# K and Q evacuated as interleaved 16-bit head pairs, with a new order per segment type, in a segment-recurrent attention kernel

## The chip, the cores and the metric

The kernel runs on one core of a Trainium2 chip. A core has TensorE (PE; its weight loads are shown as PEld), VectorE (DVE), ScalarE (ACT), GpSimd (POOL) and SyncE (SP), which issues the DMAs here. The metric is the device time of one execution in microseconds. All three runs of the kernel before lie within 0.6% of one another.

## The reference

A layer norm, a recurrent attention over segments with a memory, a residual, and a feed-forward block behind a second and third layer norm:

```python
B, S, Dm = 1, 2048, 512;  H, Dh = 32, 128;  M, seg = 8, 32
mem = mem0
for s in range(64):
    h = concat([mem, xs[s]])                       # 8 + 32 rows
    q, k, v = (einsum('btd,dhe->bhte', h, W) for W in (Wq, Wk, Wv))
    p = softmax(where(mask, q @ k^T * Dh**-0.5, -1e9))
    o = einsum('bhte,hed->btd', p @ v, Wo)
    mem = o[:, :8]                                 # the recurrence
    outs.append(o[:, 8:])
h1 = x + concat(outs)
z = layernorm(layernorm(h1))
out = h1 + gelu(z @ w1 + b1) @ w2 + b2             # F = 1792
```

Everything is 16-bit float outside of PSUM and the softmax. Each segment needs the eight memory rows of the one before it, so the 64 segments are a chain.

## The kernel before, in words

The four projection weights (4 MB each) stay in SBUF. Tokens come in 16 blocks of 128 rows, that is of four segments. A segment's 40 rows are worked on in two portions. Portion A is 32 rows: the first 24 tokens of the segment and the 8 memory rows; it must wait for the recurrence. Portion B is the last 8 tokens of each of the four segments of a block: 32 rows which do not depend on the memory and are projected once for a block, ahead of time. All 32 heads are held as two halves r = 0, 1 of 16 heads, and matmuls use the array as four column groups of 32, each for another part of the head dimension (`one_pass`, line 589: four chunks of four matmuls with 512 moving columns for one half of one projection).

What a segment s does, by the names of the parts in the order table:

- `K0, K1, Q0, Q1`: K and Q of portion A. Their result in PSUM has tokens on partitions. `kq_T` (line 631) is a DVE transpose of 32 x 32 blocks, from PSUM to the tile `kqT`, 4-byte floats. From there `k_seg` casts to `KALL` (16 bit, line 611); `q_seg` copies the memory queries scaled into `ZC` (line 612) and the 24 token queries scaled into `QA` (GpSimd, line 646). `zc_fill` (GpSimd, line 654) puts the B queries beside the memory queries in `ZC`.
- `V`: both halves together (`two_passes`, lines 601 and 367: the second half uses the weights that the first loaded), cast to `VS`.
- `SC0, SC1`: scores of the memory and B queries, into a PSUM bank prefilled with a mask (`prefill`, line 705; `sc_mm`, line 721); `sc_softmax` then runs maximum (729), exponential `EC` on ScalarE (733), reciprocal `rsc` (736), product `PC` (739) and transpose `PTC` (740).
- `PV0, PV1`: probabilities times V (751, 755), copied to `OT` (memory rows) and `OTB` (B rows).
- `WO`: the output projection in eight units of eight matmuls (832). A DVE transpose to `TT` (844) and two additions (838) make the next segment's memory rows in `hT`: this closes the recurrence.
- `SA` and `PVA`: attention of the 24 tokens, not in the recurrence: scores (779), softmax `SA`, `PA`, transpose `PTA` (789 to 795), product with V (804) in the next segment, output rows with the next but one's `WO`.
- `F0, F1`: portion B of the next block: its K in segment type 0 (s mod 4), its Q in type 1, its V in type 2, which also goes through DRAM into the layout `VBD`; in type 3 the output projection of the block before (`wo_B`). `TR` holds the transposes of layer norm (`ln1`) and residual (`nat`), which are there in types 0 and 1.

One PSUM group of four banks (`quad`) and four single banks (4 to 7, table `BANK`) are used by hand.

The order of TensorE's work is the written table `ORDER`, one for every segment (the first has `START`). All other operations are placed by a planner in the program: `Sched.schedule` sorts them by the length of the rest of their chain plus a `BONUS` per kind, then puts each into its engine's line at the earliest free time by its estimated duration (`dur`, `t_dve`, `t_act`, `t_pool`). For TensorE it also models the fetch of instructions (`FETCH_N`, `FETCH_US`). An operation made with `either` may run on several engines and takes the one that ends first by the estimates, where DVE is charged `LEAN` more. The estimates set nothing but the order and the engine; at run time each engine goes through its list in order and waits for semaphores.

After segment 63 the feed-forward block runs (lines 1083 to 1134), 128 x 512 matmuls in four rounds; its weights overwrite `WK` and its tiles `WQ` and `WV`.

Of the kernel before, what the change touches and what calls it, by code (L numbers as in the profile page):

```python
# [17 lines left out]
HOP = {"pe": 0.21, "act": 0.06, "dve": 0.05, "pool": 0.08, "sp": 2.0}  # L18
SWITCH = 0.1
OVERLAP = {"act": 0.1, "dve": 0.07, "pool": 0.05, "sp": 0.0}  # L20
DMA_SEMS = 100
FETCH_N, FETCH_US = 256, 3.5
HALVES = ("kqT", "KA", "ZCm", "QA", "VS", "nmc", "EC", "rsc", "PC", "PTC", "OTm", "KB", "QTB", "VSB")
BONUS = {"EC0": 40, "EC1": 40, "KA0": -2.1, "KB0": 7.39, "KB1": 40, "OTm0": -2.89, "OTx": -40, "PC0": 23.1, "PTC1": 40, "QA1": -40, "QTB0": 0.74,
# [3 lines left out]
LEAN = 0.36  # L28
# [3 lines left out]
ORDER = (("K0", 0, 1), ("K1", 0, 1), ("K0", 1, 2), ("K1", 1, 2), ("K0", 2, 99), ("K1", 2, 3), ("Q0", 0, 1), ("K1", 3, 99), ("Q0", 1, 99),  # L32
         ("Q1", 0, 99), ("V", 0, 1), ("SC0", 0, 99), ("V", 1, 99), ("SC1", 0, 99), ("F0", 0, 99), ("TR", 0, 99), ("PV0", 0, 99), ("SA", 0, 99),
         ("WO", 0, 3), ("PV1", 0, 99), ("WO", 3, 99), ("F1", 0, 99), ("PVA", 0, 99))
BANK = dict(K0=7, K1=5, Q0=4, Q1=7, V0=4, V1=5, SC0=6, SC1=7, F0=6, F1=4, FB=6, SA=4, WO=5)
# [23 lines left out]
class Sched:  # L59
# [79 lines left out]
    @staticmethod  # L139
    def lat(p, o):  # L140
        if p.is_dma:
            return HOP["sp"]
        if p.eng == "pe" and o.eng == "pe":
            return 0.0
        return HOP[p.eng]

    def schedule(self):
# [25 lines left out]
        def push(o):  # L173
            heapq.heappush(heap, (-o.rank - BONUS.get(o.kind, 0.0), pos[o], o.gidx, o))
# [13 lines left out]
        fetched, blocks = 0, [0.0]  # L188
        starts = {e: [] for e in ENGINES}
        for o in order:  # L190
# [5 lines left out]
            if o.eng == "pe":  # L196
                if o.prev is not None:
                    q = o.prev
                    t = max(t, q.start + q.dur + (SWITCH if q.mode != o.mode else 0.0))
                fetched += o.ni  # L200
                while fetched >= FETCH_N * len(blocks):
                    t = max(t, blocks[-1] + FETCH_US)
                    blocks.append(t)
                o.start = t
                lines["pe"].append(o)
                continue
# [150 lines left out]

MC, MR, MF = 1, 2, 3
# [14 lines left out]
def t_dve(n):  # L373
    return 0.16 + 1.042e-3 * n


def t_act(n, ps=True):
    return (0.14 if ps else 0.2) + 0.886e-3 * n


def t_pool(n):
    return 0.16 + 2.1e-3 * n


def build_kernel(nc, A_x, A_mem0, A_Wq, A_Wk, A_Wv, A_Wo, B_w1, B_b1, B_w2, B_b2, out):
# [3 lines left out]
    with st:  # L389
# [20 lines left out]
        kqT = sb("kqT", [P, 6, 512], F32)  # L410
        KALL = sb("KALL", [P, 4, H, 32])
        QTB = sb("QTB", [P, 2, H, 32])
        ZC = sb("ZC", [P, 2, H, 32])
        QA = sb("QA", [P, H, 32])
# [90 lines left out]
        S.op("dve", lambda e: e.memset(QA[:], 0.0), writes=[("QA", r) for r in range(2)], dur=0.5)  # L505
# [39 lines left out]
        def ln1(tb):  # L545
# [4 lines left out]
            S.op("dve", lambda e: e.bn_aggr(ag, stt[:, i, :]), reads=[("st", i)], writes=[("ag", i)], dur=0.15)  # L550
# [3 lines left out]
                 reads=[("xr", tb % XR), ("ag", i), ("rs", i)], writes=[("xn", i)], dur=0.38)  # L554
# [29 lines left out]
        def one_pass(lhs, reads, W, key, r, bank, rhs):  # L584

            for cc in range(DC):
# [4 lines left out]
                S.op("pe", f, reads=[(key, r, cc)] + reads, writes=[("ps", bank)], dur=0.215, mode=MC, ni=8)  # L591

        def two_passes(lhs, reads, W, key, banks, rhs):

            for cc in range(DC):
# [9 lines left out]
                S.op("pe", f, reads=[(key, r, cc) for r in range(2)] + reads, writes=[("ps", b) for b in banks], dur=0.43, mode=MC, ni=12)  # L605

        def copy2(out, src, n, ps_=True, scale_=None):

            fast = 1.0 if ps_ else 0.5
            if scale_ is None:  # L610
                return {"act": (lambda e: e.copy(out, src), t_act(n, ps_)), "dve": (lambda e: e.tensor_copy(out, src), 0.16 + 1.042e-3 * n * fast)}  # L611
            return {"act": (lambda e: e.mul(out, src, scale_), t_act(n, ps_)),  # L612
                    "dve": (lambda e: e.tensor_scalar(out, src, scale_, None, ALU.mult), 0.16 + 1.042e-3 * n * fast)}
# [16 lines left out]
        def kq_T(i, bank):  # L630
            S.op("dve", lambda e: e.transpose(kqT[:, i, :], ps[bank][:, :]), reads=[("ps", bank)], writes=[("kqT", i)], dur=t_dve(512) + 0.02)  # L631
            return kqT[:, i, :].rearrange("p (h t) -> p h t", h=16)

        def k_seg(s, r, bank):
            par, i, h0 = s % 2, r, 16 * r
            src = kq_T(i, bank)
            S.either(copy2(KALL[:, par, h0:h0 + 16, :], src, 512, False), reads=[("kqT", i)], writes=[("KA", par, r)])

        def q_seg(s, r, bank):
            par, i, h0 = s % 2, 2 + r, 16 * r  # L640
            src = kq_T(i, bank)
            z = ZC[:, par, h0:h0 + 16, :]
            dst = bass.AP(z.tensor, z.offset, [list(z.ap[0]), [64, 8], [48, 2], [1, MEM]])
            sz = src[:, :, NA:SEG].rearrange("p (a b) t -> p a b t", b=2)
            S.either(copy2(dst, sz, 128, False, scale), reads=[("kqT", i)], writes=[("ZCm", par, r)])
            S.op("pool", lambda e: e.tensor_scalar(QA[:, h0:h0 + 16, 0:NA], src[:, :, 0:NA], scale, None, ALU.mult),  # L646
                 reads=[("kqT", i)], writes=[("QA", r)], dur=1.19)

        def zc_fill(s):
# [3 lines left out]
            src = QTB[:, bk % 2, :, 8 * sg:8 * sg + 8].rearrange("p (a b) t -> p a b t", b=2)  # L653
            S.op("pool", lambda e: e.tensor_copy(dst, src), reads=[("QTB", bk % 2, q) for q in range(2)], writes=[("ZCb", par)], dur=0.45)

# [3 lines left out]
        def kq_B(bk, qk, r, bank):  # L659
            W, key = WKQ[qk]  # L660
            one_pass(*pack_b(bk), W, key, r, bank, cols_kq)
            src = kq_T(4 + r, bank)
            h0 = 16 * r
            if qk == 0:
                S.either(copy2(KALL[:, 2 + bk % 2, h0:h0 + 16, :], src, 512, False), reads=[("kqT", 4 + r)], writes=[("KB", bk % 2, r)])
            else:
                S.either(copy2(QTB[:, bk % 2, h0:h0 + 16, :], src, 512, False, scale), reads=[("kqT", 4 + r)], writes=[("QTB", bk % 2, r)])

        def v_B(bk, r, bank):
            one_pass(*pack_b(bk), WV, "WV", r, bank, cols_v)  # L670
            S.either(copy2(VSB[:, :, r, :], ps[bank][:, :].rearrange("p (i e) -> p i e", i=4), 512), reads=[("ps", bank)], writes=[("VSB", r)])
# [36 lines left out]
        def sc_mm(s, r, bank):  # L708
# [4 lines left out]
            def f(e):  # L713
                for i in range(4):
                    for j in range(4):
                        h = 16 * r + 4 * j + i
                        b0 = (reg * H + h) * 32 + 8 * sg - 8 * i
                        a0 = (par * H + h) * 32
                        rhs = bass.AP(ka.tensor, ka.offset + a0, [list(ka.ap[0]), [b0 - a0, 2], [1, 32]])
# [5 lines left out]
                 writes=[("ps", bank)], dur=0.13, mode=MC, ni=32)  # L725
# [467 lines left out]
```

## Time and profile before

| | |
|---|---|
| median of 3 runs | 899.82 us |
| lowest and highest | 896.92, 902.28 us |
| profiled execution: span from the first to the last instruction (no other time of it is given) | 898.3 us |
| busy: PE, DVE, ACT, POOL | 822.1, 652.2, 521.9, 223.7 us |
| HBM read, written | 28.98, 8.39 MB |
| mean granted TensorE clock | 0.991 |

A busy share is an average over three stages: the load of the weights with the first segment, the chain of segments, and the feed-forward block. Matmuls are pipelined and their ends are modelled, so TensorE's share says little on how much of its time is free. For the chain of segments, the useful number is the distance of the starts of two segments, and what the chain of waits passes through between them. A row of that chain reads: start, duration, engine, tile and line, number of instructions. A row of the groups reads: line, engine, operation, output and input tiles, shapes, count, then busy time and mean duration in ns, then idle time ahead of it and what ended it.

### The profile page before, as it was taken

To read this page: it belongs to the slowest core of one execution; us is meant where nothing else is said; L and a number is where in the kernel's file an instruction comes from. 1 tells how busy PE (TensorE), PEld (TensorE's weight loads), DVE (VectorE), ACT (ScalarE), POOL (GpSimd) and SP (SyncE) were. 2 spreads that over 40 slices of the span, in tenths; PEclk is the share of its full clock that TensorE was granted. 3 is DMA by queue.
4 is the path that set the end of the run, shared out by engine and by line. 5 is a ranking of instruction groups with operands and counts; after the bars stand their busy time and mean duration, and the time that the engine had idled before them with its cause. 6 is when DMAs were issued, how large, how long until landed. Compare 5 with 4: busy or idle time off the path is not lost.

```text
span 898.3 us, 47685 instructions
## 1 busy us (share of the span) xinstructions
PE 822.1 (92%) x22271; PEld 433.7 (48%) x21261; DVE 652.2 (73%) x1801; ACT 521.9 (58%) x1520; POOL 223.7 (25%) x305
## 2 busy tenths in 40 slices
PE   2578999999999999999999999999999998889998
PEld 0134455555545555545555545555555554454443
DVE  2258788888788988897888888878797878741111
ACT  1246665657566757666757655667665656534442
POOL 3023222223232323232222222222222222223100
PEclk9789999999999999999999999999999999999999
DMA  8860000000001010101010101010101110421000
GB/s 335 285 218 10 4 15 22 19 25 15 28 10 33 9 31 12 27 16 27 16 27 16 28 15 27 9 28 9 27 10 27 34 27 10 150 77 47 24 24 23
DMA packets 35301, 40.42 MB, mean 45 GB/s; under 512 B 2452, under 2 KB 31004, under 8 KB 35100
## 3 DMA queue, kind: packets, MB, share of 16 engines
q1 hardware_dynamic: 35100, 37.38, 12.8%
q8 instruction: 170, 2.79, 1.3%
q14 instruction: 31, 0.25, 0.1%
HBM read 28.98 MB, written 8.39 MB: 42 GB/s over the span
## 4 chain that ended last, share of the span: by engine, by line
PE 72%; ACT 15%; DVE 6%; DMA 3%; issue 3%; SPq 1%; POOL 0%; DVEq 0%
PE ps L589 27%; PE ps L832 15%; ACT VS L611 7%; PE ps L601 7%; PE ps L367 6%; PE ps L1083 5%; PE quad L1090 5%; ACT EC L733 4%; ACT OT L611 3%; DVE kqT L631 2%; PE quad L804 2%; PE quad L751 2%; DMA WQ<-in_A_Wq_dram 1%; DMA xr<-in_A_x_dram 1%; PE ps L721 1%
## 5 line engine op out<-in xcount | busy, mean ns | idle before, releaser
L646 POOL TENSOR_SCALAR QA<-kqT 128x384 bf16<-128x384 f32 x128 | 150.0, 1172 | 488.1 <-PE ps L589 320.0
L631 DVE STREAM_TRANSPOSE kqT<-ps 128x512 f32<-128x512 f32 x320 | 217.9, 710 | 29.2 <-PE ps L589 19.2
L832 PE MATMUL ps<-WO,OT 128*32 128x256 bf16 x4224 | 153.6, 274 | 17.6 <-issue 6.2
L611 ACT CAST KALL<-kqT 128x512 bf16<-128x512 f32 x160 | 98.6, 618 | 80.3 <-DVE kqT L631 78.9
L589 PE MATMUL ps<-WK,hT 128*32 128x512 bf16 x2048 | 133.3, 380 | 3.9 <-DVE hT L838 3.6
L589 PE MATMUL ps<-WQ,hT 128*32 128x512 bf16 x2048 | 134.0, 382 | 0.0
L611 ACT CAST OT<-quad 128x128 bf16<-128x128 f32 (+1 forms) x176 | 80.1, 455 | 82.9 <-PE quad L755 46.8
L832 PEld LDWEIGHTS ps<-WO,OT 128*32 128x32 bf16 x4224 | 95.7, 96 | 49.5 <-ACT OT L611 33.5
L601 PE MATMUL ps<-WV,hT 128*32 128x512 bf16 x1024 | 100.7, 383 | 1.0
L367 PE MATMUL ps<-WV,hT 128*32 128x512 bf16 x1024 | 99.8, 380 | 0.0
L589 PEld LDWEIGHTS ps<-WQ,hT 128*32 128x32 bf16 x2048 | 54.7, 98 | 57.7 <-DVE kqT L631 2.4
L733 ACT ACTIVATE EC<-ps,nmc 128x64 f32<-128x64 f32 x256 | 78.0, 313 | 0.8 <-DVE nmc L729 0.8
L611 ACT CAST VS<-ps 128x512 bf16<-128x512 f32 x127 | 68.2, 589 | 10.4 <-PE ps L367 3.4
L589 PEld LDWEIGHTS ps<-WK,hT 128*32 128x32 bf16 x2048 | 49.0, 96 | 48.4 <-DVE hT L838 3.3
L1086 ACT ACTIVATE WQ<-ps,b1t 128x512 bf16<-128x512 f32 x56 | 38.5, 688 | 57.2 <-PE ps L1083 56.8
L705 ACT COPY ps<-maskCF 128x128 f32<-128x128 f32 x122 | 32.8, 269 | 65.1 <-DVE kqT L631 34.6
L844 DVE STREAM_TRANSPOSE TT<-ps 128x256 f32<-128x256 f32 x66 | 29.3, 444 | 41.8 <-PE ps L832 41.8
L1134 DVE TENSOR_TENSOR WV<-quad,WV 128x512 bf16<-128x512 f32 x16 | 11.0, 690 | 66.7 <-PE quad L1090 66.7
L601 PEld LDWEIGHTS ps<-WV,hT 128*32 128x32 bf16 x1024 | 27.3, 97 | 60.9 <-DVE kqT L631 29.9
L721 PEld LDWEIGHTS ps<-KALL,ZC 128*32 128x32 bf16 x2048 | 34.3, 97 | 44.4 <-ACT ZC L612 35.1
L1090 PE MATMUL quad<-WK,WQ 128*128 128x512 bf16 x217 | 53.7, 379 | 0.9 <-DVE xr L878 0.5
L733 ACT ACTIVATION_READ_ACCUMULATOR EC<-ps,nmc 128x1 f32 x256 | 52.3, 204 | 0.0
(107 smaller groups left out, 1210.7 us busy)
## 6 DMA issues: line engine op xcount, KB each, us to landing
WV<-in_A_Wv_dram SPq DMA_DIRECT2D x4, 1024.0 KB, 6.9
WK<-in_A_Wk_dram SPq DMA_DIRECT2D x4, 1024.0 KB, 8.0
v_last<-VSB SPq DMA_DIRECT2D x64, 64.0 KB, 2.1
WQ<-in_A_Wq_dram SPq DMA_DIRECT2D x4, 1024.0 KB, 8.5
VBD<-v_last SPq DMA_DIRECT2D x64, 64.0 KB
WO<-in_A_Wo_dram SPq DMA_DIRECT2D x4, 1024.0 KB, 9.1
WK<-in_B_w_dram SPq DMA_DIRECT2D x2, 1792.0 KB, 13.2
xr<-in_A_x_dram SPq DMA_DIRECT2D x16, 128.0 KB, 2.8
```

Of the source, the lines that this page charges most:

```text
L367: return e.add_instruction(mybir.InstMatmult(name="I-%d" % (4000000 + _kept[0]), engine=mybir.EngineType.PE, start_tensor_calc=start, stop ...
L589: ins = e.matmul(ps[bank][32 * j:32 * j + 32, :], lhs(cc), rhs(W, r, cc, j), start=(cc == 0), stop=(cc == DC - 1), tile_position=(0, 32 * j))
L601: ins = e.matmul(o, l, m, start=(cc == 0), stop=(cc == DC - 1), tile_position=(0, 32 * j))
L611: return {"act": (lambda e: e.copy(out, src), t_act(n, ps_)), "dve": (lambda e: e.tensor_copy(out, src), 0.16 + 1.042e-3 * n * fast)}
L631: S.op("dve", lambda e: e.transpose(kqT[:, i, :], ps[bank][:, :]), reads=[("ps", bank)], writes=[("kqT", i)], dur=t_dve(512) + 0.02)
L646: S.op("pool", lambda e: e.tensor_scalar(QA[:, h0:h0 + 16, 0:NA], src[:, :, 0:NA], scale, None, ALU.mult), reads=[("kqT", i)], writes=[("Q ...
L721: ins = e.matmul(ps[bank][32 * j:32 * j + 32, 64 * sl:64 * sl + 64], ZC[:, par, h, :], rhs, start=False, stop=(i == 3), tile_position=(0, ...
L733: ins = e.activation(EC[:, r, sl, :], ps[bank][:, 64 * sl:64 * sl + 64], ACTF.Exp, bias=nmc[:, r, sl:sl + 1], accum_out=smc[:, r, sl:sl + 1])
L832: ins = e.matmul(ps[bank][32 * j:32 * j + 32, 0:256], lhs(slot(h)), wo_cols(h, b), start=(k == 0), stop=(k == 15), tile_position=(0, 32 * ...
L1083: ins = e.matmul(ps[bank][:, 0:SBT], W1[:, cc, fc * P:(fc + 1) * P], hnT_of(k)[:, cc, :], start=(cc == 0), stop=(cc == DC - 1))
L1086: S.op("act", lambda e: e.activation(gT[:, fc, :], ps[bank][:, 0:SBT], ACTF.Gelu_apprx_tanh, bias=b1t[:, fc:fc + 1], scale=1.0), reads=[(" ...
L1090: S.op("pe", lambda e: e.matmul(quad[:, t, :], gT[:, fc, t * P:(t + 1) * P], W2[:, fc, :], start=(fc == 0), stop=(fc == FC - 1)), reads=[" ...
```

## The change

K and Q leave PSUM first: `kq_out` copies a bank to 16 bits in a tile `kqP`, with heads 2p and 2p+1 interleaved element by element (Q is scaled on the way). `pair_T` then transposes that tile as 4-byte elements, from SBUF to SBUF, straight into `KALL`, `QTB` or the new tile `QT`. These hold two heads with a step of two elements, so the score products read their operands with that step. `QA` and its GpSimd operation are gone; `ZC` is filled from `QT` on any of three engines. V of portion A runs as two single halves, V of portion B with shared weight loads. The order table becomes four, one for each segment type, each with its own banks; `wo_B` becomes the part `FB`. The planner's constants, durations and bonuses are others, DVE's extra charge is higher, and its model of the fetch is another. PA may run on GpSimd. `hnT0` is a tile of its own instead of lying in `kqT`.

```diff
-LEAN = 0.36
+LEAN = 22.363
...
-ORDER = (("K0", 0, 1), ("K1", 0, 1), ("K0", 1, 2), ("K1", 1, 2), ("K0", 2, 99), ("K1", 2, 3), ("Q0", 0, 1), ("K1", 3, 99), ("Q0", 1, 99),
-         ("Q1", 0, 99), ("V", 0, 1), ("SC0", 0, 99), ("V", 1, 99), ("SC1", 0, 99), ("F0", 0, 99), ("TR", 0, 99), ("PV0", 0, 99), ("SA", 0, 99),
-         ("WO", 0, 3), ("PV1", 0, 99), ("WO", 3, 99), ("F1", 0, 99), ("PVA", 0, 99))
...
+          (("Q0", 0, 3), ("K0", 0, 1), ("Q0", 3, 4), ("K0", 1, 3), ("Q1", 0, 1), ("K0", 3, 4), ("Q1", 1, 4), ("K1", 0, 4), ("SC0", 0, 1),
+           ("V0", 0, 2), ("PVA", 0, 1), ("V0", 2, 4), ("SC1", 0, 1), ("V1", 0, 3), ("F0", 0, 1), ("V1", 3, 4), ("TR", 0, 1), ("PV0", 0, 1),
+           ("F0", 1, 3), ("WO", 0, 2), ("PV1", 0, 1), ("WO", 2, 8), ("SA", 0, 1), ("F1", 0, 1), ("F0", 3, 4), ("F1", 1, 4)),
...
+        kqP = sb("kqP", [P, 6, 512])
+        KALL = sb("KALL", [P, 4, KREG])
+        QTB = sb("QTB", [P, 2, 1024])
+        QT = sb("QT", [P, 2, 1024])
...
+        def pairs(t):
+            return t.rearrange("p (h t b) -> p h t b", t=32, b=2)
+
+        def kq_out(i, bank, scale_=None):
+            src = ps[bank][:, :].rearrange("p (h b e) -> p h b e", b=2, e=32)
+            dst = pairs(kqP[:, i, :]).rearrange("p h e b -> p h b e")
+            S.either(copy2(dst, src, 512, True, scale_), reads=[("ps", bank)], writes=[("kqP", i)])
+
+        def pair_T(dst, i, key):
+            S.op("dve", lambda e: e.transpose(dst.bitcast(U32), kqP[:, i, :].bitcast(U32)), reads=[("kqP", i)], writes=[key], dur=0.445)
...
         def k_seg(s, r, bank):
-            par, i, h0 = s % 2, r, 16 * r
-            src = kq_T(i, bank)
-            S.either(copy2(KALL[:, par, h0:h0 + 16, :], src, 512, False), reads=[("kqT", i)], writes=[("KA", par, r)])
+            par, i = s % 2, r
+            kq_out(i, bank)
+            pair_T(kreg(par, r), i, ("KA", par, r))
...
+            kq_out(i, bank, scale)
+            qt = QT[:, par, 512 * r:512 * r + 512]
+            pair_T(qt, i, ("QT", par, r))
...
-            S.op("pool", lambda e: e.tensor_scalar(QA[:, h0:h0 + 16, 0:NA], src[:, :, 0:NA], scale, None, ALU.mult),
-                 reads=[("kqT", i)], writes=[("QA", r)], dur=1.19)
+            src = pairs(qt)[:, :, NA:SEG, :].rearrange("p h t b -> p h b t")
+            S.either(copy2(dst, src, 128, False, pool=True), reads=[("QT", par, r)], writes=[("ZCm", par, r)])
...
-                        rhs = bass.AP(ka.tensor, ka.offset + a0, [list(ka.ap[0]), [b0 - a0, 2], [1, 32]])
+                        rhs = bass.AP(ka.tensor, ka.offset + a0, [list(ka.ap[0]), [b0 - a0, 2], [2, 32]])
...
+            pa = lambda e: e.tensor_tensor(PA[:], SA[:], bc(rsa), ALU.mult)
+            S.either({"dve": (pa, 0.42), "pool": (pa, 0.8)}, ["SA", "rsa"], ["PA"])
...
+            BANK = BANKS[sg] if s else BANK0
```

The order shown after is that of type 1; the other three have the same parts in similar places (type 0 starts Q0 and K0 in halves, type 2 runs the next block's V as one part `F`, type 3 has `FB` in place of `F0` and `F1`).

189 lines of the change are left out of this document (116 added, 73 removed), and 17 rows, old and new, of tables (BONUS, ORDER).

## The prediction

> **What bounds the kernel now.** I read the page first, then the chain of waits in a few stretches, the timeline of one segment, the windows, and the groups by form. The page shows engines that all look loaded:
>
> ```profile
> span 898.3 us, 47685 instructions
> PE 822.1 (92%) x22271; PEld 433.7 (48%) x21261; DVE 652.2 (73%) x1801; ACT 521.9 (58%) x1520; POOL 223.7 (25%) x305
> q8 instruction: 170, 2.79, 1.3%
> ```
>
> TensorE at 92% looks like the bound, but that share counts modelled matmul ends. The chain of waits gives the pace. A segment starts with the first matmuls of line 589; segment 1 starts at 61.76 and segment 63 at 773.24:
>
> ```profile
> 61.76 3.28 PE ps L589 x53
> 773.24 3.64 PE ps L589 x64
> ```
>
> So 62 periods take 711.5 us, 11.48 us each. Segments 2 to 4 carry no projection of a next block; TensorE has 32 matmuls fewer in them. One of them, segment 3, in the chain, and the start of the second score product in its timeline:
>
> ```profile
> 84.68 3.64 PE ps L589 x64
> ...
> 88.89 0.12 PE ps L721 x16
> ...
> 90.35 1.07 ACT VS L611 x2
> ...
> 92.23 0.84 PE ps L832 x24
> 93.07 0.20 PE quad L751 x16
> 93.26 0.09 PE quad L755 x4
> ...
> 93.37 0.28 ACT OT L611
> ...
> 93.69 1.09 PE ps L832 x32
> ...
> 95.73 0.82 PE ps L589 x9
> ```
> ```profile
> 90.13 0.29 PE L721 MATMUL ps<-KALL,ZC 128*32 128x64 bf16 x16
> ```
>
> It takes 95.73 - 84.68 = 11.05 us. A full segment takes little more:
>
> ```profile
> 418.52 3.57 PE ps L589 x64
> ...
> 428.56 0.86 PE ps L589 x16
> 429.42 0.30 PE quad L804 x32
> 429.72 3.57 PE ps L589 x64
> ```
>
> That is 11.20 us, with 32 more projection matmuls (2 x 0.86 us by the second row). So the recurrence sets the pace: projections, transposes, scores, softmax, PV, output projection, the new memory rows, next projections. The rest of TensorE's work hides in its gaps. Between the quiet 11.05 to 11.20 and the mean of 11.48 lie some 0.3 us a segment; where I looked at longer segments, the chain has "issue" there, TensorE waiting for nothing but its own instructions, and a long one stands behind the last segment:
>
> ```profile
> 405.01 0.68 issue
> 784.17 3.00 issue
> ```
>
> The instruction queue moved 170 packets, and 170 x 256 is 43520, against 22271 + 21261 = 43532 TensorE instructions: these are the fetches of its stream, 256 at a time. [...]
>
> **The change, part by part.** The groups that are touched, and windows that give each engine's load over one segment and over four:
>
> ```profile
> L646 POOL TENSOR_SCALAR QA<-kqT 128x384 bf16<-128x384 f32 x128 | 150.0, 1172 | 488.1 <-PE ps L589 320.0 <-DVE kqT L631 136.1 <-DVE rsa L793 27.2
> L631 DVE STREAM_TRANSPOSE kqT<-ps 128x512 f32<-128x512 f32 x320 | 217.9, 710 | 29.2 <-PE ps L589 19.2
> L611 ACT CAST KALL<-kqT 128x512 bf16<-128x512 f32 x160 | 98.6, 618 | 80.3 <-DVE kqT L631 78.9
> L612 ACT ACTIVATE ZC<-kqT 128x128 bf16<-128x128 f32 x128 | 39.3, 307 | 2.4 <-DVE kqT L631 0.8
> L844 DVE STREAM_TRANSPOSE TT<-ps 128x256 f32<-128x256 f32 x66 | 29.3, 444 | 41.8 <-PE ps L832 41.8
> L795 DVE STREAM_TRANSPOSE PTA<-PA 128x256 bf16<-128x256 bf16 x64 | 28.3, 441 | 1.5
> L794 DVE TENSOR_TENSOR PA<-SA,rsa 128x256 bf16<-128x256 f32 x64 | 26.4, 412 | 0.8
> L705 DVE COPY ps<-maskAF 128x256 f32<-128x256 f32 x63 | 25.3, 401 | 0.0
> ```
> ```profile
> core 0: us, PE busy (x) PEld busy (x) DVE busy (x) ACT busy (x) POOL busy (x), PEclk, DMA share, GB/s
> 407.28:418.45 11.17, 10.84 (x373) 6.49 (x346) 8.81 (x27) 6.52 (x21) 2.73 (x3) 1.00 0.19 49
> ...
> 407.28:452.00 44.72, 43.92 (x1360) 23.73 (x1287) 38.95 (x110) 29.53 (x92) 12.52 (x16) 1.00 0.08 21
> ```
>
> *Transposes.* Five per segment (four of K and Q, one on the mean of the next block; 320 in all). 256 elements cost 444 ns in four-byte and 441 ns in two-byte form, 512 cost 710 ns: the price follows the number of elements, not of bytes. A pair tile has 256 four-byte elements, so 710 becomes 445, and DVE gets 5 x 0.265 = 1.3 us back per segment. The ends: 0.44, or 0.71 if pairs are priced as 512.
>
> *Way out of PSUM.* Five copies of 512 elements per segment now stand ahead of the transpose, in place of 2.5 K copies (618 ns) and half a Q one behind it. No row writes every second 16-bit element. Straight VS casts out of PSUM take 1.07 for two, 0.54 each, which is the lower end; twice the 618 ns row, 1.24, is the upper. I take 0.60, near the two rows of the same size. [...]
>
> *Who does it.* The planner's charge for DVE rises from 0.36 to 22.363 us, so nearly every copy with a choice goes to ScalarE or GpSimd: the 256-wide mask prefill (0.40 on DVE) to ScalarE, PA (0.41 on DVE) to GpSimd. DVE has 38.95 / 4 = 9.7 us a segment; less 1.3, 0.4 and 0.4 that is 7.6. ScalarE has 29.53 / 4 = 7.4; plus 5 x 0.60, less 3 x 0.62, plus 0.4 it is 8.9, or 8.3 where the two memory-query copies (0.31 each) go to GpSimd. GpSimd has 12.52 / 4 = 3.1; it loses 2 x 1.17 of QA and gains PA and perhaps those copies, and stays below that. PA's delay is covered by the time to PVA, which now stands behind the next segment's SC0; without that cover it would cost what GpSimd is slower than 0.41, perhaps as much again.
>
> *The loop.* Now SC1 starts 90.13 - 84.68 = 5.45 us into a segment, behind four transposes of 0.71 in a row and nearly all of V, and 5.60 us pass from there to the next start. After: Q goes first and K1 last. 64 matmuls at 0.86 for 16 are 3.44. Then SC1 needs K1's copy, 0.60, and transpose, 0.445, and an allowance of 0.45 for three handovers: 4.93. The new order puts SC0 (0.12), half a V (0.86) and PVA (0.30) there, 4.72, so TensorE is busy meanwhile. The Q side has a step more (copy, transpose, copy to ZC), but is projected 0.86 us or more ahead. SC1: 4.95. Behind it the softmax steps stay; WO does two units before PV1 and six after, of which two run beside the 0.28 us OT copy, so four stand behind that copy where five do now (1.09): less 0.2. SA and matmuls of the next block move behind WO, where they fill the time of TT (0.44) and of the additions into hT. Loop: 4.95 + 5.60 - 0.2 = 10.35.
>
> *TensorE's own floor.* With that slack gone, its work counts: 128 projection matmuls at 0.86 for 16 are 6.88; WO, eight units at some 0.22 (1.09 for five), 1.75; scores 2 x 0.12; SA, twice the instructions of a score product, 0.24; PV 2 x 0.29; PVA 0.30: 10.0, and an allowance of 0.3 for the layer norm's and residual's transposes and for changes of mode: 10.3. V loses its shared weight loads (16 loads more a segment), the next block's V gains them. Strided operands of scores and SA could double these, 0.5 more; I take nothing for want of a row that shows a step, and keep the 0.5 in the upper bound.
>
> *Fetch.* Four segments have 1360 + 1287 = 2647 TensorE instructions now, 2640 by the code, and 2688 after: 10.5 blocks instead of 10.3. I keep 0.3 us a segment.
>
> *Collisions.* Loop (10.35) and floor (10.3) meet, and ScalarE is busy 8.3 to 8.9 of some 10.5 us in a fixed order; a copy of 0.6 ahead of EC or OT is a wait on the loop. I add 0.15.
>
> Period: 10.35 + 0.3 + 0.15 = 10.8 (bounds 10.3 and 11.3). Head, up to segment 1: 61.8, less 0.5, since QA no longer stands ahead of the ZC fill on GpSimd; the larger zeroing of KALL on DVE lies in the wait for the weights, and costs perhaps 2 if it does not. From segment 63 on: 898.3 - 773.2 = 125.1, less 0.7 for that segment; W1 waits for K's last use as before. Sum: 61.3 + 62 x 10.8 + 124.4 = 855.3. The page gives no time beside its span of 898.3; the median, 899.82, lies 1.5 above it, which I add: 857.
>
> **The rivals.** *ScalarE keeps the loop long.* What DVE no longer delays, ScalarE does: its work goes from 7.4 to as much as 8.9 a segment, and the chain already has 1.07 of VS casts ahead of EC. For it: more copies per segment, each ready when EC or OT is. Against it: the new order moves Q, K and V apart. With 0.4 more of such waits the period is 11.2: 61.3 + 694.4 + 124.4 + 1.5 = 882.
>
> *Better than that.* PVA, SA and the next block's work stand where the fetch and the loop wait, so that the 0.3 and the 0.15 vanish: 10.35, 829. Against it: "issue" also stands in the middle of WO (405.01), which stays.
>
> *Slower: fetch becomes the bound.* A segment has 2.58 blocks now and 2.63 after. If blocks cannot come faster than at the present mean, 11.48 / 2.58 = 4.45 us, the period becomes 11.7, and the time 912. It decides above 11.48 / 2.63 = 4.37 us a block. Against it: the segment from 407.28 has 373 + 346 = 719 TensorE instructions, 2.8 blocks, in 11.17 us, 4.0 a block, which would allow 10.5 here.
>
> *Slower: the step of four bytes is dear.* At twice the 618 ns, ScalarE needs 8.3 + 3.2 = 11.5 us a segment; with the 0.3 of fetch, 11.8 and 919. It decides from about 1.2 us a copy. Nothing in the rows speaks for it, and none excludes it.
>
> **How the numbers follow.** Forecast (period 10.6 to 11.0, 845 to 870): 0.50. ScalarE keeps the loop long (870 to 893): 0.20. Better (825 to 845): 0.16. No net effect, within 0.5% (4.5 us, about what a measurement of this kernel can tell from no change): 0.05. Fetch bound 0.05, dear step 0.04. So faster 0.86, same 0.05, slower 0.09. The range, 834 to 884, holds the forecast and more than half of "better" and of the ScalarE rival: about 0.75 to 0.8.
>
> **What would show it.** Right: 320 transposes of 256 four-byte elements near 445 ns; 320 copies out of PSUM near 0.6 us, mostly on ScalarE; no QA group; starts of segments near 10.8 apart, those of 2 to 4 near 10.4; DVE down to some 70% and ScalarE up to some 80% in the middle. Wrong: copies over 1 us; transposes over 0.6; EC or OT behind kqP copies in the chain; more "issue" in the chain than before; starts still 11.05 apart in segments 2 to 4, which would say that the loop was not shortened.

## The result, and the profile after

The changed kernel takes 879.31 us (median of 4 runs, 875.88 to 880.64), the kernel before 900.22 (4 runs, 896.92 to 902.28): a ratio of 0.9764, with a 95% interval of 0.9735 to 0.9794. It is faster by 2.4%. The prediction said 857, faster by 4.8%: the sign came true, and the time lies inside the range of 834 to 884, but the gain is half of what was forecast. The profiled execution took 880.2 us, with a span of 878.3.

The page of the changed kernel, where the rows of the engines and the instruction queue answer to those of before, and where the last row shown gives the shares of the chain of waits:

```profile
span 878.3 us, 48583 instructions
PE 813.7 (93%) x22285; PEld 444.2 (51%) x22045; DVE 529.0 (60%) x1651; ACT 626.7 (71%) x1624; POOL 145.5 (17%) x353
q8 instruction: 174, 2.85, 1.3%
PE 70%; DVE 12%; ACT 11%; DMA 3%; issue 2%; SPq 1%; POOL 0%; DVEq 0%
```

VectorE gave up 123 us of work (652.2 to 529.0) and ScalarE took on 105 (521.9 to 626.7). TensorE's busy time fell by 8 (822.1 to 813.7), and the span by 20.

The chain's rows in which segment 1 and segment 63 start:

```profile
63.01 2.15 PE ps L619 x36
...
751.68 3.41 PE ps L619 x57
```

62 periods take 688.7 us, 11.11 each, where they took 711.5 (11.48). The head is 63.0 against 61.8, the part from segment 63 on 126.6 against 125.1. So the whole gain is in the chain of segments, 22.8 us, and head and tail give 2.7 back.

The touched groups by form:

```profile
L645 ACT ACTIVATE kqP<-ps 128x512 bf16<-128x512 f32 x160 | 119.4, 757 | 28.6 <-PE ps L619 27.2
L644 ACT CAST kqP<-ps 128x512 bf16<-128x512 f32 x160 | 117.0, 740 | 13.3 <-PE ps L619 10.9
L644 ACT CAST VS<-ps 128x512 bf16<-128x512 f32 x128 | 74.8, 586 | 2.6 <-PE ps L619 1.4 <-PE ps L396 1.1
L672 DVE STREAM_TRANSPOSE KALL<-kqP 128x256 uint32<-128x256 uint32 x160 | 70.1, 438 | 26.4 <-ACT kqP L644 24.1
L672 DVE STREAM_TRANSPOSE QT<-kqP 128x256 uint32<-128x256 uint32 x128 | 56.7, 443 | 21.9 <-ACT kqP L645 18.8
```

The transposes cost 438 and 443 ns, as the sum had it. All 320 copies out of PSUM run on ScalarE, and they cost 740 and 757 ns. The third row is a copy of the same size, from PSUM to the same 16 bits, on the same engine: 586. It differs from the second in where it writes: in one run of elements, where the pair copy leaves out every second element of the stretch it writes and comes back for it.

Four segments in the windows, to compare with the four from 407.28 before, in the same columns:

```profile
405.86:450.05 44.19, 43.54 (x1368) 24.40 (x1340) 31.85 (x103) 35.74 (x97) 7.59 (x19) 1.00 0.08 23
```

ScalarE is now busier than VectorE: 35.74 against 31.85, where it was 29.53 against 38.95. In the chain, a segment of the quiet kind (segment 3, to the start of the next at 94.47) and, below it, the early part of a full segment of type 0:

```profile
84.04 2.15 PE ps L619 x36
...
86.22 0.77 ACT kqP L644
...
87.01 0.27 ACT ps L754
87.28 0.68 ACT kqP L645
87.95 0.59 ACT kqP L644
...
88.57 0.27 ACT ps L754
88.84 0.64 ACT EC L783 x4
...
94.47 1.04 PE ps L619 x13
...
407.79 0.76 ACT kqP L645
408.55 0.59 ACT kqP L644
409.13 0.22 ACT ZC L641
409.36 0.68 ACT kqP L645
```

Segment 3 takes 94.47 - 84.04 = 10.43 us, where it took 11.05. But three pair copies and two mask prefills in a row stand between its first matmuls and the exponentials `EC`: ScalarE, not the transposes, now carries the chain there, and in the full segment too. What that costs is not read from the chain alone: with cheaper copies (e2 below) segment 3 takes the same 10.43 us, with a chain of TensorE's matmuls in the place of ScalarE's copies.

### The profile page after: what moved, and what is told of

Read it like the earlier page. It is cut to its first block, busy times and chain, and to the rows that moved or that the text cites. A ratio compares the mean times of both kernels' runs of the same rounds, so it can differ in the third digit from the quotient of the medians.

```text
span 878.3 us, 48583 instructions
## 1 busy us (share of the span) xinstructions
PE 813.7 (93%) x22285; PEld 444.2 (51%) x22045; DVE 529.0 (60%) x1651; ACT 626.7 (71%) x1624; POOL 145.5 (17%) x353
## 4 chain that ended last, share of the span: by engine, by line
PE 70%; DVE 12%; ACT 11%; DMA 3%; issue 2%; SPq 1%; POOL 0%; DVEq 0%
PE ps L619 30%; PE ps L884 16%; PE ps L1162 6%; PE quad L1169 6%; PE quad L801 3%; ACT kqP L645 3%; ACT EC L783 2%; PE ps L771 2%; ACT kqP L644 2%; PE ps L631 2%; PE ps L830 2%; PE quad L856 1%; DVE PC L789 1%; PE ps L396 1%; DVE opT L912 1%
## 5 line engine op out<-in xcount | busy, mean ns | idle before, releaser
L619 PE MATMUL ps<-WQ,hT 128*32 128x512 bf16 x2048 | 154.8, 383 | 4.7 <-DVE hT L890 4.6
L619 PE MATMUL ps<-WK,hT 128*32 128x512 bf16 x2048 | 152.4, 379 | 0.0
L619 PE MATMUL ps<-WV,hT 128*32 128x512 bf16 x2016 | 147.3, 380 | 0.0
L645 ACT ACTIVATE kqP<-ps 128x512 bf16<-128x512 f32 x160 | 119.4, 757 | 28.6 <-PE ps L619 27.2
L644 ACT CAST kqP<-ps 128x512 bf16<-128x512 f32 x160 | 117.0, 740 | 13.3 <-PE ps L619 10.9
L845 POOL TENSOR_TENSOR PA<-SA,rsa 128x256 bf16<-128x256 f32 x64 | 40.1, 627 | 379.5 <-DVE rsa L844 263.2
L672 DVE STREAM_TRANSPOSE KALL<-kqP 128x256 uint32<-128x256 uint32 x160 | 70.1, 438 | 26.4 <-ACT kqP L644 24.1
L672 DVE STREAM_TRANSPOSE QT<-kqP 128x256 uint32<-128x256 uint32 x128 | 56.7, 443 | 21.9 <-ACT kqP L645 18.8
L842 ACT ACTIVATE SA<-SA 128x256 f32<-128x256 f32 x64 | 26.5, 414 | 45.3 <-DVE SA L841 43.6
L642 POOL COPY ZC<-QT 128x128 bf16<-128x128 bf16 x112 | 33.0, 295 | 104.3 <-DVE QT L672 103.6
```

The lines of the kernel that those rows point to most:

```text
L619: ins = e.matmul(ps[bank][32 * j:32 * j + 32, :], lhs(cc), rhs(W, r, cc, j), start=(cc == 0), stop=(cc == DC - 1), tile_position=(0, 32 * j))
L642: "pool": (lambda e: e.tensor_copy(out, src), t_pool(n))}
L672: S.op("dve", lambda e: e.transpose(dst.bitcast(U32), kqP[:, i, :].bitcast(U32)), reads=[("kqP", i)], writes=[key], dur=0.445)
L845: pa = lambda e: e.tensor_tensor(PA[:], SA[:], bc(rsa), ALU.mult)
```

## The experiments

Three theories. **The price of the copy:** the order does what was forecast, and 62 periods are longer than forecast because each of the 320 copies takes 0.75 us, not 0.60, in an engine that became the bound. **The work on ScalarE as such:** ScalarE has more copies in a fixed order, whatever one costs. **TensorE** and the fetch of its stream set the period, and the copies lie beside them. A fit of the order to exact durations may lie behind all of them, since the planner arranges the queues by estimates.

**e1: the same copy with a plain write.** It reads the bank as before and writes `kqP` in one run of elements.

```diff
-            dst = pairs(kqP[:, i, :]).rearrange("p h e b -> p h b e")
+            dst = kqP[:, i, :].rearrange("p (h b e) -> p h b e", b=2, e=32)
```

> The kernel after, in the same order on every engine, but the copy of K and Q out of PSUM writes its 512 elements one behind the other, so the heads of a pair are not interleaved and K and Q hold other values than the reference's. Theory A (the dear copy): after the change the copies take 740 to 757 ns where the plain VS cast takes 586, five a segment, and the waits for scores and probabilities that break TensorE's work come from that. With the plain write the copies fall to about 0.59 us, segments 2 to 4 from 10.5 to about 10.2, full segments from 11.1 to about 10.8 on the mean: 860 us. Theory B (TensorE is full): full segments stand on TensorE's own work of 10.7 to 10.85; then the copies fall to 0.59 all the same and segments 2 to 4 shorten, but full segments keep 11.0 or more and the time stays above 873 us.

**e2: the step on the reading side.** The pairs are made by reading PSUM with a step of 32 floats; the write is plain, and the values are those of the change.

```diff
-            src = ps[bank][:, :].rearrange("p (h b e) -> p h b e", b=2, e=32)
-            dst = pairs(kqP[:, i, :]).rearrange("p h e b -> p h b e")
+            src = ps[bank][:, :].rearrange("p (h b e) -> p h e b", b=2, e=32)
+            dst = pairs(kqP[:, i, :])
```

> The kernel after, but the copy reads PSUM with the step (head 2p, head 2p+1, next element: 32 floats apart) and writes the interleaved pairs one behind the other; the values are the same. If the price of the copy comes from the stepped 16-bit write, it falls to about 0.59 us here too and the time is that of the plain write. If a stepped pattern costs on the PSUM side as well, it stays at 0.75 us or more and the time is 879 us or more. I hold both for equally likely.

Measured: 864.24 us for e1 (863.51 to 865.63; ratio to the kernel before 0.9624, 0.9609 to 0.9640) and 863.42 for e2 (861.08 to 865.10; 0.9620, 0.9599 to 0.9640). The page of e2, the starts of its segments 1 and 63 in the chain, and its groups:

```profile
span 859.1 us, 48569 instructions
PE 81%; DVE 8%; ACT 4%; DMA 3%; issue 2%; SPq 1%; POOL 0%; DVEq 0%
```
```profile
59.93 2.12 PE ps L619 x33
...
733.02 2.99 PE ps L619 x51
```
```profile
L645 ACT ACTIVATE kqP<-ps 128x512 bf16<-128x512 f32 x160 | 94.3, 593 | 30.6 <-PE ps L619 29.6
L644 ACT CAST kqP<-ps 128x512 bf16<-128x512 f32 x160 | 93.7, 585 | 23.2 <-PE ps L619 17.9
```

The copies take 585 and 593 ns in both, and in e2 the 62 periods take 673.1 us, 10.86 each. The traces of the change, e1 and e2 have the same operations in the same order on VectorE, ScalarE and GpSimd, so nothing but the copy differs. The step in the write costs 0.155 to 0.164 us a copy, and 688.7 - 673.1 = 15.6 us of the 62 periods; e8 below, read as a second run of e2, has 674.9 and gives 13.8. Not every segment pays: segments 1 and 2 fall from 10.54 and 10.50 to 10.30 and 10.31, segment 3 stays at 10.43. ScalarE's share of the chain falls from 11% to 4%, TensorE's rises from 70% to 81%. In e1 K and Q hold other values, in e2 they hold those of the change, and the times agree: it is the form of the write that costs, and nothing that hangs on the data. e2 is also a version that beats both kernels, by 1.8% and 3.8%.

**e6: the price of each form by itself.** e2 with thirty copies of a bank ahead of the first segment, three each of five forms on ScalarE and on VectorE.

```diff
+        plain, half = fl[:, 0:512], fl[:, 0:1024].rearrange("p (n x) -> p n x", x=2)[:, :, 0]
...
+        for _ in range(3):
+            S.op("act", lambda e: e.copy(plain, b7), reads=[("ps", 7)], writes=["scr"], dur=0.6)
+            S.op("act", lambda e: e.copy(half, b7), reads=[("ps", 7)], writes=["scr"], dur=0.75)
...
```

> The kernel with the stepped read, with thirty copies of 512 elements from a PSUM bank added at the start, where ScalarE and DVE wait for weights: write plain, every second, every fourth 16-bit element, the interleaved write of the change, and the stepped read with a plain write, three of each on ScalarE and on DVE. If the step of the 16-bit write is the price on ScalarE: plain 0.59, every second 0.75, interleaved 0.75, stepped read 0.59; if it is the short runs of 32 elements, every second stays at 0.59. Where the price goes with the distance, every fourth is dearer still than every second; where it is a write of half a word, it is the same. DVE: plain 0.69, the others unknown to me; 0.69 if its writes do not mind the step.

In the diff, `fl` is the tile `hnT0` and `b7` a PSUM bank; three more forms and the same five on VectorE follow. The whole run took 874.62 us, once: the copies delay the start (segment 1 at 70.0 us for 59.9 in e2). The groups of its first 40 us. Lines 1027 to 1031 are ScalarE, 1033 to 1037 VectorE, each in the order plain, every second element, every fourth, pairs by a stepped write, pairs by a stepped read (the last form's row on VectorE is 1037):

```profile
L1027 ACT CAST hnT<-ps 128x512 bf16<-128x512 f32 x3 | 1.8, 585 | 0.1
L1028 ACT CAST hnT<-ps 128x512 bf16<-128x512 f32 x3 | 2.2, 729 | 0.1
L1029 ACT CAST hnT<-ps 128x512 bf16<-128x512 f32 x3 | 3.9, 1296 | 0.1
L1030 ACT CAST hnT<-ps 128x512 bf16<-128x512 f32 x3 | 2.2, 724 | 0.1
L1031 ACT CAST hnT<-ps 128x512 bf16<-128x512 f32 x3 | 1.8, 585 | 0.1
L1033 DVE CAST hnT<-ps 128x512 bf16<-128x512 f32 x3 | 2.1, 691 | 5.0 <-ACT hnT L1031 4.9
L1034 DVE CAST hnT<-ps 128x512 bf16<-128x512 f32 x3 | 2.2, 726 | 0.1
L1035 DVE CAST hnT<-ps 128x512 bf16<-128x512 f32 x3 | 3.9, 1292 | 0.1
L1036 DVE CAST hnT<-ps 128x512 bf16<-128x512 f32 x3 | 2.1, 715 | 0.1
L1037 DVE CAST hnT<-ps 128x512 bf16<-128x512 f32 x3 | 2.1, 692 | 0.1
```

Plain 585 ns on ScalarE; with a step of four bytes 729, of eight bytes 1296. The pair write is a step of four bytes taken twice, and costs the same, 724. The step of 32 floats in the read costs nothing here: 585 against 585, and 692 against 691 on VectorE. With a step of four bytes the 512 elements are spread over 2 KB per partition and took 726 to 729 ns, with one of eight bytes over 4 KB and took 1292 to 1296, alike on both engines, which differ where the write is plain (585 and 691). What sets these prices is not shown.

**e3 and e4: the two halves of the change alone.** e3 is the kernel before, with its order, planner and units, and the new layout. e4 is the changed kernel, with its four orders, banks and planner, and the layout of before (`kqT`, `QA`, transposes out of PSUM). e5 is e3 with the stepped read of e2.

```diff
 e3, against the kernel before:
-            src = kq_T(i, bank)
-            S.either(copy2(KALL[:, par, h0:h0 + 16, :], src, 512, False), ...)
+            kq_out(i, bank)
+            pair_T(kreg(par, r), i, ("KA", par, r))
 ...
 e4, against the changed kernel: the same lines the other way
```

> The kernel before, its order table, banks, planner and charges kept, with the interleaved pairs alone (copy, four-byte transpose, QT in place of QA, stepped operands of the score products). Theory A: K still comes first and Q last, and the Q side now has copy 0.75, transpose 0.44 and the copy to ZC, so the second score product starts no earlier than the 5.45 us of before; DVE's relief alone is worth little: 890 to 900 us. Rival: DVE was the cause of the waits, and the layout alone brings most of the gain: 880 to 885 us.

> The kernel after, its four orders, banks, planner and charges, with the layout of before (4-byte transpose of 512 elements out of PSUM, then casts; QA on GpSimd). Theory A: Q first and K last, SA and the next block's work behind WO shorten the loop without the layout as well, but four transposes of 0.71 on DVE stand in a row: 885 to 893 us. Rival: the order needs the layout; with DVE as loaded as before and the copies all on ScalarE it is no faster or slower than before: 900 us or more.

> The layout alone in the order of before (956 us, segments 2 to 4 at 11.95 us), now with the copy that reads PSUM with the step and writes plainly. Theory A: there the copies of K0, K1, Q0, Q1 stand in a row on ScalarE ahead of the last transpose and the copy to ZC, at 0.755 each, and each 0.16 saved shortens the loop: four of them take 0.6 off segments 2 to 4, 11.3, and with the same off the others the time falls to about 915 us, still above before. Rival: the loop there is long for other reasons (the order of the softmax copies on ScalarE), and the time stays above 940 us.

Measured: e3 956.23 us (ratio 1.0647, 1.0623 to 1.0671), e4 988.19 (1.1001, 1.0981 to 1.1021), e5 935.52 in its one run. Each half by itself is slower than the kernel before. e3 came out slower than either of its forecasts (900 at most), e4 on the side of its rival, e5 between its two (about 915, above 940). Their chains tell where, by the shares on the page of e3 first, then those of e4:

```profile
PE 44%; ACT 42%; DVE 7%; DMA 3%; issue 2%; SPq 1%; POOL 0%; DVEq 0%
```
```profile
PE 62%; DVE 26%; ACT 5%; DMA 3%; issue 3%; SPq 1%; POOL 0%; DVEq 0%
```

In e3 the four copies of a segment's K and Q stand in ScalarE's queue ahead of `EC`, and ScalarE carries 42% of the chain (period 12.38 us); there the plain write of e5 brings 20.7 us. In e4 VectorE gets transposes of 0.71 us again under order tables and bonuses that were fitted to 0.445, and carries 26% (12.81 us). It would be wrong to read these as prices of the halves, as e7 shows.

**e7: the planner told the true price.** The changed kernel, its copy still writing with the step; only the estimate by which the planner orders the queues is set from 0.585 to 0.74.

```diff
-            S.either(copy2(dst, src, 512, True, scale_), reads=[("ps", bank)], writes=[("kqP", i)])
+            alts = {k: (fn, 0.74 if k == "act" else dur) for k, (fn, dur) in copy2(dst, src, 512, True, scale_).items()}
+            S.either(alts, reads=[("ps", bank)], writes=[("kqP", i)])
```

> The kernel after, with the interleaved write, and the planner told that such a copy takes 0.74 us on ScalarE instead of 0.585; nothing else is changed, so only the order of the other engines and the choice of engines may move. Theory A (the price itself): the copies stay at 0.74 to 0.76 and the time at 875 to 885 us. Rival (the plan was fitted to a wrong price, and its order is what costs): 868 us or less.

Measured: 946.83 us (945.65 to 947.99; ratio 1.0535, 1.0498 to 1.0572), 67.5 slower than the change, which neither forecast had. The copies cost the same (745 and 748 ns), but the plan is another: VectorE's order differs from the change's, and ScalarE now has 65 of the 128 `ZC` copies, where it had 16. A few rows of its chain:

```profile
402.96 0.45 DVE KALL L673
...
403.44 0.25 DVE opT L891
...
403.70 0.26 DVE opT L891
...
403.97 0.46 DVE QT L673
```

Two `opT` operations here stand in VectorE's queue between a transpose of K and one of Q that a score product waits for. This is one place; how the 67.5 us divide among the moved operations is not shown. The time hangs on the plan as a whole: one truer estimate, with no new fit of the other constants, costs some four times the 15.6 us of the step itself. So how the gain divides between layout and order stays open: no fit for either half alone was made.

**e9: TensorE's stream shifted by half a block.** e2 with 64 small matmuls ahead of the first segment, 128 instructions with their weight loads, so that the boundaries of the blocks of 256 fall elsewhere (the trace of e2 has 22271 + 22045 = 44316 TensorE instructions and 174 packets in the instruction queue; 44316 / 256 is 173.1). e8 was meant to do this with 128 idle instructions.

```diff
+        def extra(e):
+            for _ in range(64):
+                ins = e.matmul(ps[7][0:32, 0:8], ident[:, 0:32], ident[:, 0:8], ...)
+            return ins
+        S.op("pe", extra, reads=["ident"], writes=[("ps", 7)], dur=0.01, mode=MC, ni=0)
```

> The kernel with the stepped read, the order on every engine the same, with 128 instructions that do nothing added to TensorE's stream before its first matmuls, where it waits for weights: half a fetch block. Four segments have 10.5 blocks, and in the run without them every second group of four is longer (segments of type 3 at 10.38 and 11.3 in turn, type 2 at 10.38 and 11.05, type 0 at 10.67 and 11.36). Theory F (the fetch of instructions makes the long ones): the long and the short groups change places, and the time stays within 3 us of 863. Rival (two-block buffers or the plan make them): they stay where they are.

> The kernel with the stepped read, with 64 small matmuls and their weight loads (128 real instructions, half a fetch block) in TensorE's stream while it waits for the first weights; the order on every engine is the same otherwise. Theory F (the fetch makes the long groups): the groups of four segments that are long without them (for instance type 3 at 11.3, type 0 at 11.36) become short and the others long; the time stays within 3 us of 863. Rival (two-block buffers or the plan): they stay where they are.

e8 took 863.32 us, and its trace has the 48569 instructions and the 174 packets of e2: the idle instructions do not show in it, and it is read here as a second measurement of e2. As such it shows how far segments vary from run to run with no change that shows: segment 27, of type 3, takes 11.55 us in e2 and 10.70 in e8, and the median of type 2 (over segments 5 to 56, as all medians here) is 10.38 and 10.76.

e9 took 861.12 (860.81 to 861.89; 0.9582, 0.9567 to 0.9597). What agrees in e2 and e8 and changes in e9 is the effect of the shift. Of type 3, segments 11, 19, 47 and 55 take 11.3 to 11.8 us in e2 and e8 and 10.38 or 10.39 in e9; segments 7, 23, 31 and 51 take 10.4 to 10.8 in e2 and e8 and 11.2 to 11.8 in e9. The other six of type 3 (15 to 59) stay, move less, or differ between e2 and e8 already. The output projection of segment 19 and what follows it, in the chain of e2, then of e8, then of e9:

```profile
260.08 2.53 PE ps L884 x88
...
262.65 0.73 issue
```
```profile
264.41 2.53 PE ps L884 x88
...
266.98 0.79 issue
```
```profile
262.25 1.46 PE ps L884 x48
...
263.74 0.46 DVE TT L896
```

In e2 and e8 TensorE stops at the same place, for 0.73 and 0.79 us; in e9 the chain goes from the output projection straight to the transpose for the next memory rows. The order on every engine is the same, and only the places in the blocks differ, which points to the fetch as what makes these segments long. The packets of the instruction queue in the trace of e2 agree: its 62 periods have 11 "issue" rows over 0.2 us, and each ends 1.3 to 1.5 us behind the end of such a packet. But the shift only moves the stops: the mean period stays (10.86 and 10.85). The 11 rows of e2 come to 5.8 us, some 0.1 us a segment. Of type 0, segments 12, 20 and 28 are long in e2, e8 and e9 alike (11.3 to 12.3), so those have another cause.

**e10, e11, e12: what holds the period of 10.86.** All are e2 with one edit: each transpose in two halves (e10), the memory queries' copy to `ZC` kept off ScalarE (e11), and the next block's projections of K and Q cut from 512 to 128 columns from block 2 on (e12).

```diff
 e10
-            S.op("dve", lambda e: e.transpose(dst.bitcast(U32), kqP[:, i, :].bitcast(U32)), ...)
+            S.op("dve", lambda e: [e.transpose(dst.bitcast(U32)[:, k:k + 128], kqP[:, i, :].bitcast(U32)[:, k:k + 128]) for k in (0, 128)][1], ...)
 e11
+            alts = copy2(dst, src, 128, False, pool=True)
+            del alts["act"]
 e12
-            one_pass(*pack_b(bk), W, key, r, bank, cols_kq)
+            one_pass(*pack_b(bk), W, key, r, bank, cols_kq, 512 if bk < 2 else 128)
```

In e12 `one_pass` takes the number of columns as a new argument.

> The kernel with the stepped read, each transpose of 256 four-byte elements split into two of 128, in the same order: 0.31 each by the PTC row, so 0.6 in place of 0.44, near the 0.71 of before. It prices what the four-byte transposes bring. Theory A (the chain K1, copy, transpose, scores is on the loop, and with TensorE full only part of it shows): one transpose of 0.17 more per segment at least, up to three that stand in a row: 62 x 0.17 to 62 x 0.4, 873 to 888 us. Rival (DVE has room and TensorE is full): below 868 us.

> The kernel with the stepped read; the copies of the memory queries may no longer go to ScalarE, where 16 of 128 went, all in segments of type 0, six of which waited about 0.7 us for them. If the planner's order survives that, 855 to 862 us. Rival (an order that was fitted to the exact durations does not survive any change of them, as with the planner that was told 0.74): 870 us or more.

> The kernel with the stepped read, order the same; from block 2 on the K and Q projections of the next block (types 0 and 1) move only 128 of 512 columns, so that TensorE has about 1.2 us less to do in a segment of type 0 or 1 (eight groups of 0.2155 go to about a quarter, if 128 columns take a quarter); three quarters of these K and Q values are left out. Theory B (TensorE's own work now sets the full segments): type 1 falls from 10.66 to the loop's 10.3 to 10.45, types 2 and 3 stay at 10.38. Rival (the loop alone sets them): all stay.

e10 took 865.15 us (864.20 to 866.51; 0.9626, 0.9609 to 0.9643), 1.7 above e2's median, with intervals of the ratio that overlap. Its halves take 286 ns each but overlap: the busy time of the 160 K transposes is 78.6 us in place of 69.8 in e2, so each grew by 0.05 us, a third of what was meant. The time is below the rival's 868, but with so small an edit it tells little.

e11 took 862.13 (0.9605, 0.9577 to 0.9632): no difference to e2 that can be measured, and type 0 stays long (median 11.39). The 16 `ZC` copies of the change that ran on ScalarE, one of them in the chain at 409.13, are not the cause.

e12 took 856.87 in its one run. Its type 1 goes from 10.66 to 10.39, its type 0 from 11.34 to 11.02, and none of segments 5 to 56 gets shorter than 10.38. Types 2 and 3 were expected at 10.38; their medians are 10.86 and 10.81. They were 10.38 and 10.77 in e2 and 10.76 and 10.74 in e8, so runs of one program differ as much, and no effect of the edit on them is shown. Type 1 has 10.66 or 10.67 in e1, e2, e6, e8, e9, e10 and e11 alike. So in e2 the full segments of type 1 are bound by the work of TensorE. The chain of e2 says the same: segment 33, of type 1, has only matmuls from its start to the second score product:

```profile
405.29 4.33 PE ps L619 x80
...
411.03 0.13 PE ps L771 x14
```

Why type 0 has segments of 10.67 and of 11.3 us: not the fetch (e9), not the `ZC` copies (e11), only in part the next block's projections (e12). VectorE's timeline in e2 shows a difference between a short one (segment 16) and, below it, a long one (segment 20):

```profile
222.97 0.45 DVE L672 STREAM_TRANSPOSE QT<-kqP 128x256 uint32<-128x256 uint32 x1
...
225.30 0.59 DVE L912 TENSOR_TENSOR opT<-TTB 64x128 bf16<-64x128 f32 x2
```
```profile
265.85 0.91 DVE L912 TENSOR_TENSOR opT<-TTB 64x128 bf16<-64x128 f32 x2
266.77 0.45 DVE L672 STREAM_TRANSPOSE QT<-kqP 128x256 uint32<-128x256 uint32 x1
```

Line 912 holds the two additions of `wo_B`, the output rows of the block before. In segments 12, 20, 28, 36, 44 and 52 the planner put them ahead of the segment's first transpose of Q, and the chain passes through them there; in 8, 16, 24, 32, 40, 48 and 56 it put them behind all four transposes, and the chain there holds nothing but TensorE's matmuls and its "issue" rows. The same order stands in the change itself, where segments 16 and 24 take 11.23 us and 20 and 28 take 11.7. That this order is the cause is read from the chain; no run moved the two additions.

## Why the prediction was half right

**The step that failed is "Way out of PSUM".** It set 0.60 us for a copy, near the two rows of that size, between ends of 0.54 and 1.24; it is 0.74 to 0.757. That is the term of the sum that was mis-sized: it charged nothing for the step in the write. For a plain write 0.60 was right (589 ns in the `VS` row of the kernel before, 585 and 593 in e2); the step adds 0.155 to 0.164. The prediction gave the reason itself: "No row writes every second 16-bit element." It chose between the ends by the rows nearest in size, 0.54 and 0.62, which were near in size but not in the form of the write. That the step is free, as the 0.60 has it, is shown by no run: on ScalarE a write with a step of four bytes took 724 to 757 ns and one with a step of eight 1296, where a plain write took 585 to 593.

**What followed from it** is the rival "ScalarE keeps the loop long", which was given 882 us and a chance of 0.20; the time is 879.31. Its mechanism is the one seen: pair copies in a row ahead of `EC`. Its cause was put as the number of copies, though, and the runs show that the price decides: with the same copies at 0.59 (e2), ScalarE has 4% of the chain, and the time is 863.42.

The account of the span: 878.3 against a forecast of 855.3 is 23.0 more. The 62 periods make 688.7 - 669.6 = 19.1 of it, the head 1.7, the tail 2.2. Of the 19.1, 15.6 go with the step in the write. In the prediction's own sum the loop holds one copy, K1's, so 0.155 more would have made 62 x 0.155 = 9.6; the rest, some 6 us (4 by e8), is what copies in a row on ScalarE cost beyond it, which the sum had under "Collisions". With that step gone (e2) the sum holds to 3.8 us: 859.1 against 855.3, with periods 3.5 over, the tail 1.7 over, and the head 1.4 under. That it holds so closely is in part luck, as "Fetch" and "Collisions" show below.

The other steps, one by one:

- *Transposes:* 0.445 forecast, 0.431 to 0.443 measured, all 320 with 256 elements. Right.
- *Who does it:* VectorE 31.85 / 4 = 8.0 us a segment for a forecast of 7.6; ScalarE 35.74 / 4 = 8.9 for 8.3 to 8.9, at the upper end with five copies 0.15 dearer; 112 of 128 `ZC` copies and all of `PA` on GpSimd, at 7.59 / 4 = 1.9. `PA` takes 627 ns there and its delay is covered: GpSimd's share of the chain is 0%.
- *The loop:* 10.35 forecast. Segment 3 takes 10.43, and in the timeline its second score product starts 5.08 us behind the segment's start (forecast 4.95) and 5.35 before the next (forecast 5.40):

```profile
89.12 0.30 PE L771 MATMUL ps<-KALL,ZC 128*32 128x64 bf16 x16
```

- *TensorE's floor:* 10.3 forecast. In e2 the shortest full segments of types 2 and 3 take 10.38, but type 1 takes 10.66 and is held there by TensorE (e12), so for it the floor was 0.36 too low. The charge of nothing for the strided operands holds: a score product takes 193 ns before and 196 after, one of `SA` 178 and 179, and their weight loads 97 and 96, 93 and 95.
- *Fetch:* 0.3 kept, about 0.1 found in e2. The trace of before had said so: its "issue" rows over 0.2 us come to 8.1 us in the 62 periods, 0.13 each, so the 0.3 between its quiet and its mean segments was only in part fetch. The instruction queue moved 174 packets, and e9 shows the stall where it falls. That fetch would become the bound did not come true: with 10.86 us a segment in e2 and the forecast's 2.63 blocks, a block comes every 4.13 us, below the 4.37 from which it would have decided.
- *Collisions:* 0.15 added. It was too little by about what fetch was too much: e2's mean of 10.86 lies within 0.06 of the forecast period of 10.8, so these two errors nearly cancel. What the runs show in its place are TensorE's work in type 1 and the order of VectorE's additions in type 0.

Two of the marks named ahead separate the cases as they should: copies near 0.6 us were wanted and were not there, and `kqP` copies ahead of `EC` in the chain were named as a mark of a wrong forecast, and were there. "Starts still 11.05 apart in segments 2 to 4" did not come true; they are 10.43 to 10.50 apart.

## What to carry to other kernels

When a layout needs two values side by side, put the step on the side of the reading in PSUM, not on that of the writing in SBUF: for ScalarE the first cost nothing here (585 ns, as plain) and the second 0.14 to 0.16 us for 512 elements (for VectorE, whose plain copy took 691 ns, 0.02 to 0.04). When a cost is bounded by rows, let the nearest row be the one nearest in form (what is stepped, and on which side), not in size, and work out the sum once with the engine that takes on the work at the dearer price, to see whether it becomes the bound. And in a kernel whose queues are arranged by estimated durations, an edit of one estimate is a change of the whole order: e7 lost 67.5 us by a truer number, so parts of such a change can't be priced by undoing them one at a time.

## What the runs showed of the hardware

- Writing 512 16-bit elements per partition from PSUM with a step of four bytes took 729 ns on ScalarE and 726 on VectorE, with a step of eight bytes 1296 and 1292; plain it took 585 and 691 (e6). The stepped prices are nearly the same on both engines, the plain ones are not.
- Reading PSUM with a step of 32 floats cost nothing on either engine (585 and 692 ns, plain 585 and 691, in e6).
- A shift of TensorE's instruction stream by 128 instructions turned segments of 11.3 us into ones of 10.38 (segment 19) and lengthened others as much (segment 51, 10.38 to 11.35). And with no shift that shows in the trace segment 27 took 11.55 us in one run (e2) and 10.70 in another (e8). A measurement of one segment may say more on where the blocks of 256 fall, or on the run, than on the edit.
- Stepped operands cost TensorE nothing that shows: score products with a step of two elements took 196 ns for 193, those of `SA` 179 for 178.
- Two transposes of 128 elements, 286 ns each, overlapped to 0.49 us of busy time (e10), where one of 256 took 0.44 (e2).
